# Chunked attention and a two-expert router on one core: attention and routing rewritten in a fixed engine order

## The chip, the core and the metric

One core of a Trainium2 chip runs the whole program in one launch. The metric is device time in microseconds, from the first to the last work of the core, as the median of several executions; lower is better. The core has five engines that work side by side and wait for each other by semaphores: TensorE (PE; its weight loads are PEld), VectorE (DVE), ScalarE (ACT), GpSimd (POOL) and SyncE (SP), and 16 DMA engines that all queues share. Each engine takes its instructions in order. A program on one core has no second core to wait for.

## What is computed

```python
for c in range(S // 32):                      # q, k, v: (4, 8, 768, 64), float32
    ctx = [max(0, 32*c - 16), min(S, 32*c + 32 + 8))
    k_full = concat(mem_k, k[:, :, ctx])      # 8 memory rows, up to 56 context rows
    a = softmax(q[:, :, chunk c] @ k_full.T / 8)
    out[:, :, chunk c] = a @ concat(mem_v, v[:, :, ctx])
x = out.transpose(0, 2, 1, 3).reshape(3072, 512)
nl = x @ w_gate + log1p(exp(x @ w_noise)) * noise   # (3072, 8)
for each token: its two largest nl choose two experts, with softmax weights g
y = sum over the two: g * (relu(x @ w1[e]) @ w2[e])  # w1: (8, 512, 1024), w2: (8, 1024, 512)
```

## The kernel before

Two stages follow each other, and between them tokens are sorted by the pair of experts that they chose.

**Attention.** `NPAIR` = 16 steps `n`: 4 batches by 4 pairs of heads (head `hp` on partitions 0 to 63, head `hp + 4` on 64 to 127). `load_group` (L253) brings float32 q, k and v for two pairs by POOL's queue, one group ahead of use, and broadcasts the 8 memory rows of v to all 24 chunks by SP's queue (L282). `qkT` (L333) turns q and k with 12 float32 transposes (L342), four ACT copies bring them to bf16 (L343), and POOL writes the two margins of kT (L344, L345). `scores` (L348) makes 48 small matmuls for the context (L356) and 48 for the memory (L362) into one PSUM tile per head, and for each head apart a maximum, a subtraction (DVE, L367, L369) and an exponential (ACT, L370). `probT` turns P (L377) and copies it (L379). `cast_v` (L285) makes bf16 of v, by turns on DVE and POOL (L290, L292). `mix` (L384) multiplies with v (48 matmuls, L394), divides (L398, L399) and writes bf16 rows of x.

**Routing.** After each batch `dispatch` (L126) turns x (L133, L135), makes the logits (L137), finds the top two (L139 to L157), the pair's bucket among `NB` = 28 (L163 to L170), its rank in the bucket by matmuls with triangular ones (L173 to L186), the slot (L200 to L204), and POOL scatters each tile of 128 rows of x, with gates and token number behind it, to its slots in DRAM (L227). A bucket has 128 slots; the rows beyond go to 32 spill rows. All slots were first filled with blanks by one large DMA (`fill_blank`, L87). The order within each engine comes from a scheduler that goes by priority, not from the order of the lines.

**Experts.** For each expert `e`, `load_w` (L434) casts w1 and w2 to bf16 on the way (two buffers each). `fetch` (L448) reads a bucket's 128 rows by SP, turns them (L453, one PSUM buffer `p_t`), copies them (L454) and takes gates and token numbers (POOL, L455, L456). `hidden` (L504) multiplies w1 with the 7 buckets of `e` (groups of 4 and 3, with the spill rows) and applies relu on ACT (L516) and DVE (L518). Then per bucket 8 matmuls with w2 (L547); the first expert of a pair scales into `acc` (ACT, L551), the second adds to it (DVE, L553), and POOL scatters the 128 rows to the output (L554). The spill rows follow (L560 to L565), at the end their scatter (L566), and a loop (L575) for more spill, which these inputs do not enter.

Of the kernel before, what the change touches and what calls it, by code (L numbers as in the profile page):

```python
# [17 lines left out]
Act = mybir.ActivationFunctionType  # L18


@with_exitstack
def kernel(
# [20 lines left out]

# [3 lines left out]
    assert moe_w1.shape == (E, Dm, F)  # L47
    assert moe_w2.shape == (E, F, Dm)
# [15 lines left out]
    SPILL = 32
    I32 = mybir.dt.int32
    XC = Dm // 2
    META = 8
    ROW = XC + META
    NROW = NB * CAP + N
    PAD_TOK = 4 * N  # L70
# [4 lines left out]

    xd = nc.dram_tensor("x_by_pair", [NROW, ROW], I32, kind="Internal").ap()
    xd_tile = dram_disjoint_views(xd, NP)
    out_tile = dram_disjoint_views(out, NB + 1)

    rcon = ctx.enter_context(tc.tile_pool(name="rcon", bufs=1))  # L80
    rpool = ctx.enter_context(tc.tile_pool(name="rpool", bufs=2))

    def fill_blank():
        blank = rcon.tile([128, ROW], I32, name="blank")
        nc.vector.memset(blank, 0)
        nc.vector.memset(blank[:, XC:XC + 1].bitcast(F32), float(PAD_TOK))
        nc.sync.dma_start(  # L87
            out=xd[:NB * CAP, :].rearrange("(p g) r -> p g r", p=128),
            in_=blank.rearrange("p (o r) -> p o r", o=1).to_broadcast([128, NB, ROW]),
        )  # L90
        nc.sync.dma_start(out=xd[NB * CAP:NB * CAP + SPILL, :], in_=blank[:SPILL, :])

    upper = rcon.tile([128, 128], BF16, name="upper")
    nc.gpsimd.memset(upper, 1.0)
    nc.gpsimd.affine_select(out=upper, in_=upper, compare_op=Alu.is_gt, fill=0.0, base=0, pattern=[[1, 128]], channel_multiplier=-1)
    ones = rcon.tile([128, 128], BF16, name="ones")
    nc.gpsimd.memset(ones, 1.0)

    ramp_i = rcon.tile([128, NB], I32, name="ramp_i")
    nc.gpsimd.iota(ramp_i, pattern=[[1, NB]], base=0, channel_multiplier=0)  # L100
    ramp = rcon.tile([128, NB], F32, name="ramp")
    nc.vector.tensor_copy(ramp, ramp_i)
    code = rcon.tile([128, E], F32, name="code")
    nc.vector.tensor_scalar(out=code, in0=ramp[:, :E], scalar1=-1.0, scalar2=float(E), op0=Alu.mult, op1=Alu.add)
    tok_i = rcon.tile([128, NP], I32, name="tok_i")
    nc.gpsimd.iota(tok_i, pattern=[[128, NP]], base=0, channel_multiplier=1)

    wgn_f = rcon.tile([128, KP, 2, E], F32, name="wgn_f")
    nc.sync.dma_start(out=wgn_f[:, :, 0, :], in_=moe_w_gate.rearrange("(kp p) e -> p kp e", p=128))
    nc.sync.dma_start(out=wgn_f[:, :, 1, :], in_=moe_w_noise.rearrange("(kp p) e -> p kp e", p=128))  # L110
    wgn = rcon.tile([128, KP, 2 * E], BF16, name="wgn")
    nc.vector.tensor_copy(wgn, wgn_f.rearrange("p k t e -> p k (t e)"))
    nz_all = rcon.tile([128, NP, E], F32, name="nz_all")
    nc.sync.dma_start(out=nz_all, in_=moe_noise.rearrange("(t p) e -> p t e", p=128))

    seen = rcon.tile([128, NB], BF16, name="seen")
    nc.gpsimd.memset(seen, 0.0)
    seen_ov = rcon.tile([128, 1], BF16, name="seen_ov")
    nc.gpsimd.memset(seen_ov, 0.0)
    n_spill_i = rcon.tile([128, 1], I32, name="n_spill_i")  # L120
    n_spill = rcon.tile([128, 1], F32, name="n_spill")

    def bc(ap, n):
        return ap.rearrange("p (t o) -> p t o", o=1).to_broadcast([128, BT, n])

    def dispatch(b, xrow):  # L126
        T = lambda name, shape, dt=F32: rpool.tile(shape, dt, name=name)
        t0 = b * BT
        ps_l = psR.tile([128, BT, 2 * E], F32, name="ps_l", tag="rt")
        for t in range(BT):  # L130
            p_x = psT.tile([128, KP, 128], BF16, name="p_x", tag="tr")
            for kp in range(KP):
                nc.tensor.transpose(out=p_x[:, kp, :], in_=xrow[:, t, kp * 64:(kp + 1) * 64].bitcast(BF16), identity=identb)  # L133
            xt = rpool.tile([128, KP, 128], BF16, name="xt")
            nc.scalar.copy(xt, p_x)  # L135
            for kp in range(KP):
                nc.tensor.matmul(out=ps_l[:, t, :], lhsT=xt[:, kp, :], rhs=wgn[:, kp, :], start=(kp == 0), stop=(kp == KP - 1))  # L137
        ns = T("ns", [128, BT, E])
        nc.scalar.activation(out=ns, in_=ps_l[:, :, E:], func=Act.Exp)  # L139
        nc.scalar.activation(out=ns, in_=ns, func=Act.Ln, bias=1.0)  # L140
        nl = T("nl", [128, BT, E])
        nc.vector.tensor_mul(nl, ns, nz_all[:, t0:t0 + BT, :])
        nc.vector.tensor_tensor(out=nl, in0=nl, in1=ps_l[:, :, :E], op=Alu.add)

        codeb = code.rearrange("p (o e) -> p o e", o=1).to_broadcast([128, BT, E])
        c = [T("c1", [128, BT]), T("c2", [128, BT])]
        m = [T("m1", [128, BT]), T("m2", [128, BT])]
        eq = T("eq", [128, BT, E])
        nl2 = T("nl2", [128, BT, E])
        for i, src in enumerate((nl, nl2)):  # L150
            nc.vector.tensor_reduce(out=m[i], in_=src, axis=AX, op=Alu.max)
            nc.vector.tensor_tensor(out=eq, in0=src, in1=bc(m[i], E), op=Alu.is_equal)
            nc.vector.tensor_mul(eq, eq, codeb)
            nc.vector.tensor_reduce(out=c[i], in_=eq, axis=AX, op=Alu.max)
            if i == 0:
                nc.vector.tensor_tensor(out=eq, in0=codeb, in1=bc(c[0], E), op=Alu.is_equal)
                nc.vector.scalar_tensor_tensor(out=nl2, in0=eq, scalar=-1e30, in1=nl, op0=Alu.mult, op1=Alu.add)  # L157

# [485 lines left out]
```

## Time and profile before

| what | us |
|---|---|
| median of 3 runs (482.41, 482.56, 488.23) | 482.56 |
| span of the profiled execution, first to last instruction | 478.0 |
| median less that span (start and end around it) | 4.56 |

The page shows one profiled execution, in microseconds from the start of its span. Its own time outside the profiler is not listed apart; its span and the 4.56 us around it are taken for it, so that sums made on its durations are compared with 482.56 us.

### The profile page before, as it was taken

Reading aid. Unit: us, or ns where it says so; the run is one execution under the profiler, and the core shown is the slowest. Engines: PE = TensorE matmul, PEld = TensorE weight load, DVE = VectorE, ACT = ScalarE, POOL = GpSimd, SP = SyncE. Lnnn points to the kernel's source line nnn. Section 1 sums busy time; section 2 is a strip of 40 time slices with the busy share of each in tenths; the row PEclk is TensorE's granted clock in tenths of the full one; section 3 lists DMA queues with packets and bytes.
Section 4 is the critical chain, followed back from the end, with each engine's and each line's share of the span. In section 5 each row is a group of like instructions: output and inputs, shape, how many; then the busy total and the mean of one; then the engine's idle time right before and its main releaser. Section 6 shows DMA issues by size and latency. Waiting matters only on the chain. (4 is left out here: it accounts for less than half of the span.)

```text
span 478.0 us, 10565 instructions
## 1 busy us (share of the span) xinstructions
PE 322.1 (67%) x4481; PEld 199.1 (42%) x4497; DVE 171.6 (36%) x493; ACT 127.4 (27%) x233; POOL 165.2 (35%) x267
## 2 busy tenths in 40 slices
PE   2225555454555484510399599599899999999992
PEld 2114444344444363400254265264455545454541
DVE  1014437565346468440230231231324323333341
ACT  2212232623352244500033123132231223131200
POOL 9756562179317810651100100200303140313133
PEclk9999985965556566555599789899999999999998
DMA  7999998139922800299315615715835665761112
GB/s 136 261 294 282 293 224 178 48 99 209 237 55 86 203 6 3 71 191 226 86 33 90 121 36 88 137 30 88 172 61 123 100 148 87 161 110 73 40 57 86
DMA packets 41842, 60.06 MB, mean 126 GB/s; under 512 B 14170, under 2 KB 29623, under 8 KB 41792
## 3 DMA queue, kind: packets, MB, share of 16 engines
q0 software_dynamic: 23008, 49.93, 47.0%
q1 hardware_dynamic: 18464, 9.35, 8.9%
q8 instruction: 37, 0.61, 0.6%
q14 instruction: 13, 0.11, 0.1%
q10 hardware_dynamic: 320, 0.07, 0.1%
HBM read 62.73 MB, written 14.47 MB: 162 GB/s over the span
## 5 line engine op out<-in xcount | busy, mean ns | idle before, releaser
L512 PE MATMUL ps_h<-xTb,w1t 128*128 128x384 bf16 (+4 forms) x832 | 112.8, 292 | 1.0 <-DVE xTb L454 1.0
L547 PE MATMUL ps_y<-w2t,ht 128*128 128x512 bf16 x432 | 97.1, 379 | 0.9
L512 PEld LDWEIGHTS <-w1t 128*128 128x128 bf16 x832 | 62.0, 99 | 44.3 <-issue 3.7
L516 ACT ACTIVATE ht<-ps_h 128x512 bf16<-128x512 f32 x64 | 38.2, 597 | 133.6 <-PE ps_h L512 133.6
L547 PEld LDWEIGHTS <-ht 128*128 128x128 bf16 x448 | 43.2, 98 | 51.5
L518 DVE TENSOR_SCALAR ht<-ps_h 128x416 bf16<-128x416 f32 x64 | 37.9, 592 | 65.2 <-PE ps_h L512 65.2
L554 POOL DMA_INDIRECT out_dram<-acc,tid x28 | 28.1, 1003 | 78.4 <-DVE acc L553 41.0
L553 DVE SCALAR_TENSOR_TENSOR acc<-ps_y,meta,acc 128x512 f32<-128x512 f32 x28 | 21.0, 751 | 54.5 <-PE ps_y L547 54.5
L227 POOL DMA_INDIRECT x_by_pair<-xrow,slot_i x24 | 24.5, 1023 | 37.3 <-DVE vwin L292 15.1
L551 ACT ACTIVATE acc<-ps_y,meta 128x512 f32<-128x512 f32 x28 | 19.2, 687 | 61.3 <-PE ps_y L547 61.3
L342 PE MATMUL p_t<-ident,qn 128*128 128x128 f32 x96 | 22.5, 393 | 13.8 <-DMA qn<-in_q_dram 11.8
L370 ACT ACTIVATE P<-sd 128x384 bf16<-128x384 f32 x32 | 15.7, 522 | 54.4 <-DVE sd L369 54.4
L343 ACT CAST qT<-p_t 128x384 bf16<-128x384 f32 x32 | 15.1, 479 | 42.8 <-PE p_t L342 42.4
L356 PE MATMUL ps_s<-kT,qT 64*32 64x56 bf16 x768 | 13.9, 219 | 16.7 <-POOL kT L344 5.7
L437 POOL DMA_DIRECT2D w1t<-in_moe_w_dram x8 | 6.4, 801 | 54.1 <-PE ps_h L512 54.1
L280 POOL DMA_DIRECT2D vf<-in_v_dram x16 | 22.8, 1426 | 6.2 <-issue 5.6
L342 PE MATMUL p_t<-ident,kn 128*128 128x128 f32 x96 | 21.0, 380 | 5.6 <-DMA kn<-in_k_dram 5.6
L455 POOL COPY meta<-xl 128x8 f32<-128x8 f32 x28 | 5.3, 190 | 55.7 <-DMA xl<-x_by_pair 55.6
L367 DVE TENSOR_REDUCE mx<-ps_s 128x6 f32<-128x384 f32 x32 | 16.4, 550 | 21.6 <-PE ps_s L362 18.8
L453 PE MATMUL p_t<-identb,xl 128*128 128x128 bf16 x112 | 13.0, 250 | 15.3 <-DMA xl<-x_by_pair 10.5
L342 PEld LDWEIGHTS p_t<-ident,qn 128*128 128x128 f32 x96 | 16.3, 203 | 15.3 <-issue 12.5
L362 PE MATMUL ps_s<-mkT,qT 64*32 64x8 bf16 x768 | 10.4, 176 | 16.8 <-issue 16.8
(139 smaller groups left out, 379.3 us busy)
## 6 DMA issues: line engine op xcount, KB each, us to landing
vf<-in_v_dram POOLq DMA_DIRECT2D x14, 672.0 KB, 14.4
w1t<-in_moe_w_dram POOLq DMA_DIRECT2D x8, 1024.0 KB, 8.4
w2t<-in_moe_w_dram POOLq DMA_DIRECT2D x8, 1024.0 KB, 11.1
qn<-in_q_dram POOLq DMA_DIRECT2D x14, 384.0 KB, 11.8
kn<-in_k_dram POOLq DMA_DIRECT2D x14, 384.0 KB, 11.8
x_by_pair<-blank SPq DMA_DIRECT2D x1, 3696.0 KB
xl<-x_by_pair SPq DMA_DIRECT2D x28, 132.0 KB
vf<-in_mem_v_dram SPq DMA_DIRECT2D x32, 48.0 KB
```

The costliest lines, as they stand in the source:

```text
L227: nc.gpsimd.indirect_dma_start(out=xd_tile[t0 + t], out_offset=bass.IndirectOffsetOnAxis(ap=slot_i[:, t:t + 1], axis=0), in_=xrow[:, t, :] ...
L280: nc.gpsimd.dma_start(out=dst[:, lo:hi, :], in_=src(lo, hi - lo))
L342: nc.tensor.transpose(out=p_t[:, t * 128:(t + 1) * 128], in_=src[:, hp % HV, g * HT + t, :, :], identity=ident)
L367: nc.vector.tensor_reduce(out=mx, in_=ps[hh], axis=AX, op=Alu.max)
L370: nc.scalar.activation(out=P[:, :, hh, :], in_=sd, func=Act.Exp, scale=scale)
L512: nc.tensor.matmul(out=ps_h[:, off:off + n], lhsT=w1t[:, kp, f * 128:(f + 1) * 128], rhs=rhs(kp), start=(kp == 0 and i == 0), stop=(kp == ...
L516: nc.scalar.activation(out=ht[:, f, lo:hi], in_=ps_h[:, :hi - lo], func=Act.Relu)
L518: nc.vector.tensor_scalar(out=ht[:, f, lo:hi], in0=ps_h[:, :hi - lo], scalar1=0.0, scalar2=None, op0=Alu.max)
L547: nc.tensor.matmul(out=ps_y, lhsT=ht[:, f, j * CAP:(j + 1) * CAP], rhs=w2t[:, f, :], start=(f == 0), stop=(f == FB - 1))
L551: nc.scalar.activation(out=acc[p], in_=ps_y, func=Act.Copy, scale=gate)
L553: nc.vector.scalar_tensor_tensor(out=acc[p], in0=ps_y, scalar=gate, in1=acc[p], op0=Alu.mult, op1=Alu.add)
L554: nc.gpsimd.indirect_dma_start(out=out_tile[p], out_offset=bass.IndirectOffsetOnAxis(ap=tid[p][:, 0:1], axis=0), in_=acc[p], in_offset=Non ...
```

## The change

All of the function is rewritten and emitted as written, engine by engine in the order of the lines (`manual_schedule`); nothing reorders it. What changes:

- **Loads.** POOL's DMAs cast q, k and v to bf16 on the way. q and k come as six rows of a head per piece (partition `p` holds tokens `6p` to `6p+5`, 1,536 source bytes), v as before in rows of 64 elements (256 source bytes, now 128 bytes written). `cast_v`, the margins of kT, the broadcast of the memory rows and the blank fill are gone; v's memory rows are one small load (`memv`). Each group is loaded two groups ahead (three buffers).
- **Heads.** A pair is two neighbouring heads. q and k are turned by 24 bf16 matmuls with the identity, and the copy puts tokens back in order; the memory part of scores and of P·V takes 12 matmuls over 128 queries each instead of 48 over 32. Maximum, subtraction, exponential, reciprocal and product each take both heads in one operation. Missing context is set to -1e30 by small matmuls.
- **Loop.** One iteration `i` holds: turn P of pair `i-1`, turn q and k of pair `i+2`, P·V of `i-1`, scores of `i+1`, turn x and logits of `i-2`; routing steps are put behind it, at most three per iteration (a fourth where a batch ends).
- **Routing.** Rows of x go to DRAM in token order, by SP. The table of tokens per bucket and rank is made by one-hot products on PE (`Rn`, `oht`, `ohp`, `ps_t`), summed over batches. One ACT table is loaded ahead for all functions.
- **Experts.** POOL gathers the rows of a bucket by that table (`gather`) for the next expert; they are turned between the matmuls with w2 of the present one (`turn`). Weights have three buffers, relu takes ACT and DVE by turns with four PSUM buffers, and the spill rows come after the second bucket.

```diff
+            qg = ap_.tile([128, 2 * GP, SJ * D], BF16, name="qg", bufs=3)
+            kg = ap_.tile([128, 2 * GP, SJ * D], BF16, name="kg", bufs=3)
+            vg = ap_.tile([128, GP, ncnk, D], BF16, name="vg", bufs=3)
...
+            for dst, src in ((qg, q), (kg, k)):
+                nc.gpsimd.dma_start(out=dst[:, hs, :], in_=src[b, h0:h0 + 2 * GP][hs].rearrange("h (p j) d -> p h (j d)", p=128))
...
+                        nc.gpsimd.dma_start(
+                            out=vg[p0 + j:p0 + j + nj, x, c:c + n, :],
+                            in_=bass.AP(v.tensor, v.offset + (hd * S + c * chunk + j - left_ctx) * D, [[D, nj], [chunk * D, n], [1, D]]))
...
+        new_group(0)
+        load_qk(0, 0)
+        identb = const.tile([128, 128], BF16, name="identb")
+        make_identity(nc, identb)
+        load_v(0, 0)
...
+        def qkT_pe(n):
+            g, i = divmod(n, GP)
+            qg, kg, _ = groups[g]
+            SH = SJ // 2
+            for nm, src in (("qT", qg), ("kT", kg)):
+                dst = ap_.tile([128, 128, SJ], BF16, name=nm, bufs=3)
+                for x in range(2):
+                    p_t = psT.tile([128, SH, 128], F32, name="p_t", tag="tr")
+                    for j in range(SH):
+                        for hh in range(2):
+                            nc.tensor.matmul(out=p_t[64 * hh:64 * hh + 64, j, :], lhsT=src[:, 2 * i + hh, (SH * x + j) * D:(SH * x + j + 1) * D],
+                                             rhs=identb, start=True, stop=True)
+                    nc.scalar.copy(dst[:, :, SH * x:SH * (x + 1)], p_t.rearrange("d j p -> d p j"))
...
+        def scores_pe(n):
+            b, hp = divmod(n, HP)
+            qT, kT = st[n]["qT"], st[n]["kT"]
+            ps = psS.tile([128, 2, 512], F32, name="ps_s")
+            for u in range(BT):
+                for hh in range(2):
+                    hs = slice(64 * hh, 64 * hh + 64)
+                    nc.tensor.matmul(out=ps[:, hh, u * CTX + WIN:(u + 1) * CTX], lhsT=qT[hs, 128 * u:128 * (u + 1)],
+                                     rhs=mkT[hs, hp, b * n_mem:(b + 1) * n_mem], start=True, stop=True)
...
+            mx = ap_.tile([128, 2, BT], F32, name="mx")
+            nc.vector.tensor_reduce(out=mx, in_=st[n]["ps"], axis=AX, op=Alu.max)
...
+            po = psO.tile([128, 2, 512], F32, name="ps_o")
+            OW = D + 2
+            for u in range(BT):
+                for hh in range(2):
+                    hs = slice(64 * hh, 64 * hh + 64)
+                    nc.tensor.matmul(out=po[:, hh, u * OW:u * OW + D + 1], lhsT=PT[hs, u, :], rhs=memv[hs, n, :D + 1],
+                                     start=(u == 0), stop=False, skip_group_check=True)
...
+        def xT_pe(n):
+            b, hp = divmod(n, HP)
+            p_x = psT.tile([128, BT, 128], BF16, name="p_x", tag="tr")
+            for t in range(BT):
+                nc.tensor.transpose(out=p_x[:, t, :], in_=xrows[b][:, t, hp * 64:(hp + 1) * 64].bitcast(BF16), identity=identb)
+            xt = ap_.tile([128, BT, 128], BF16, name="xt")
+            nc.scalar.copy(xt, p_x)
+            st[n]["xt"] = xt
+        def logits_pe(n):
+            b, hp = divmod(n, HP)
+            if hp == 0:
+                logits[b] = psL.tile([128, BT, 2 * E], F32, name="ps_l")
+            for t in range(BT):
+                nc.tensor.matmul(out=logits[b][:, t, :], lhsT=st[n]["xt"][:, t, :], rhs=wgn[:, hp, :],
...
+                nc.sync.dma_start(out=rows(lo, ROW, xd_part[b]), in_=xrows[b][:, :, lo:ROW])
...
+                for t in range(BT):
+                    nc.vector.tensor_scalar(out=Rn[:, t, :], in0=ramp, scalar1=rank_all[:, t0 + t:t0 + t + 1], scalar2=None, op0=Alu.is_equal)
...
+            def s6():
+                ps_t = psT.tile([128, NB], F32, name="ps_t", tag="tr")
+                for t in range(BT):
+                    for j, o in enumerate(R["ohs"]):
+                        nc.tensor.matmul(out=ps_t, lhsT=R["Rn"][:, t, :], rhs=o[:, t, :], start=(t == 0 and j == 0),
...
+        for i in range(NPAIR + 2):
+            if 0 <= i - 1 < NPAIR:
+                PT_pe(i - 1)
+            if i < NPAIR:
+                max_dve(i)
+            if i + 2 < NPAIR:
+                qkT_pe(i + 2)
+            if 0 <= i - 1 < NPAIR:
+                PT_dve(i - 1)
+            if i < NPAIR:
+                sub_dve(i)
+            if 0 <= i - 1 < NPAIR:
+                PV_pe(i - 1)
+            if i + 1 < NPAIR:
+                scores_pe(i + 1)
+            if 0 <= i - 1 < NPAIR:
+                mult_dve(i - 1)
+                if i - 1 == NPAIR - 2:
+                    nc.sync.dma_start(
+                        out=xd_part[B][(B - 1) * S:, :XC - 64].rearrange("(t p) r -> p t r", p=128),
+                        in_=xrows[B - 1][:, :, :XC - 64])
+            if 0 <= i - 2 < NPAIR:
+                xT_pe(i - 2)
+                logits_pe(i - 2)
+                if (i - 2) % HP == HP - 1:
+                    pending.extend(route((i - 2) // HP))
+                    steps(1)
+            if i % GP == 0 and i // GP >= 1 and i // GP + 2 < NG:
+                g = i // GP + 2
+                new_group(g)
+                if g == NG - 1:
+                    for x in range(GP):
+                        load_qk(g, x)
+                        load_v(g, x)
+                else:
+                    load_qk(g)
+                    load_v(g)
+            if i == 2 * (NG - 2) - 1:
+                load_w1(0)
+                load_w2(0)
+                load_w1(1)
+            if i < NPAIR:
+                steps(3)
+        steps(len(pending))
...
+        def gather(p):
+            xl = ld.tile([128, ROW], I32, name="xl")
+            nc.gpsimd.indirect_dma_start(
+                out=xl, out_offset=None, in_=xd, in_offset=bass.IndirectOffsetOnAxis(ap=gidx[:, p:p + 1], axis=0),
+                bounds_check=N - 1, oob_is_err=True)
+            got[p] = xl
...
+        def turn(p):
+            xl = got[p]
+            p_t = psX.tile([128, KP, CAP], BF16, name="p_t")
             for kp in range(KP):
+                nc.tensor.transpose(out=p_t[:, kp, :], in_=xl[:, kp * 64:(kp + 1) * 64].bitcast(BF16), identity=identb)
+            nc.vector.tensor_copy(xTv[:, :, p, :], p_t)
...
+                parts = [big[:2], big[2:], small]
+                off = 0
+                for x, ps in enumerate(parts):
+                    for p in ps:
+                        turn(p)
+                    if x == 2:
+                        turn_spill()
+                    first(W1[e], ht, off, ps, x == 2)
+                    off += len(ps) * CAP
...
+            nxt = list(plan[e + 1]) if e + 1 < E else []
+            for p in nxt:
+                gather(p)
+            if e + 2 < E:
+                load_w1(e + 2)
+            order = big + small
+            for j, p in enumerate(order):
+                second(e, p, ht, j, W2[e])
+                for _ in range(2 if j else 0):
+                    if nxt:
+                        turn(nxt.pop(0))
+                if j == 1:
+                    second_spill(e, ht, W2[e])
...
+            while nxt:
+                turn(nxt.pop(0))
+            if e + 2 < E:
+                load_w2(e + 2)
```

`route` also has steps s1 to s5 (top two, one-hot `oh` by shifted products, rank, gates) and s7, s8 (adding the table, counting what was seen). After the loop the table becomes gather indices (`gidx`), and the spill rows get theirs by 25 and 96 small matmuls on PE, which stand ahead of the first `turn`.

## Rows read from the trace of the kernel before

**Rows 1.** The page, part 1: busy time of each engine and instructions.
```profile
span 478.0 us, 10565 instructions
PE 322.1 (67%) x4481; PEld 199.1 (42%) x4497; DVE 171.6 (36%) x493; ACT 127.4 (27%) x233; POOL 165.2 (35%) x267
```

**Rows 2.** Windows by stage: length, busy per engine, PEclk, DMA share, GB/s.
```profile
37.20:194.00 156.80, 85.42 (x2744) 70.77 (x2743) 86.59 (x291) 56.49 (x117) 73.74 (x102) 0.67 0.59 145
194.00:237.40 43.40, 8.19 (x96) 6.15 (x86) 10.44 (x58) 6.42 (x11) 17.03 (x32) 0.50 0.75 154
237.40:469.30 231.90, 218.89 (x1615) 114.70 (x1628) 70.45 (x123) 57.46 (x92) 44.96 (x85) 0.95 0.46 93
```

**Rows 3.** Timeline of PE, attention: start, duration [idle before, releaser].
```profile
37.25 0.59 PE L356 MATMUL ps_s<-kT,qT 64*32 64x56 bf16 x48 [3.94 <-POOL kT L344]
...
40.85 0.82 PE L377 MATMUL p_p<-identb,P 128*128 128x128 bf16 x6
...
179.59 0.51 PE L377 MATMUL p_p<-identb,P 128*128 128x128 bf16 x6
...
191.68 0.82 PE L377 MATMUL p_p<-identb,P 128*128 128x128 bf16 x6
```

**Rows 4.** Windows around the last two of rows 3; columns as in rows 2.
```profile
178.00:181.00 3.00, 2.29 (x53) 1.73 (x52) 0.00 (x0) 2.62 (x7) 0.00 (x0) 1.00 0.00 0
190.00:193.00 3.00, 1.38 (x15) 1.03 (x15) 2.76 (x14) 0.70 (x2) 0.00 (x0) 0.50 0.00 0
```

**Rows 5.** Waits: total us, times, longest us ("issue": nothing the profile shows).
```profile
PE ps_s L362 <- issue: 16.8, 5, 5.4
...
PE ps_o L394 <- issue: 5.9, 2, 5.2
```

**Rows 6.** Groups by line: busy us, mean ns of one, idle before.
```profile
L367 DVE TENSOR_REDUCE mx<-ps_s 128x6 f32<-128x384 f32 x32 | 16.4, 550 | 21.6 <-PE ps_s L362 18.8 <-PE ps_o L394 2.7
...
L370 ACT ACTIVATE P<-sd 128x384 bf16<-128x384 f32 x32 | 15.7, 522 | 54.4 <-DVE sd L369 54.4
L343 ACT CAST qT<-p_t 128x384 bf16<-128x384 f32 x32 | 15.1, 479 | 42.8 <-PE p_t L342 42.4
...
L379 DVE COPY PT<-p_p 128x768 bf16<-128x768 bf16 x16 | 8.9, 556 | 12.4 <-PE p_p L377 12.4
...
L186 DVE TENSOR_REDUCE rank<-rk 128x6 f32<-128x168 f32 x4 | 1.3, 326 | 0.1
```

**Rows 7.** Windows: float32 loads in attention, a casting weight load.
```profile
42.00:44.00 2.00, 0.02 (x1) 0.00 (x0) 0.27 (x1) 0.00 (x0) 2.00 (x3) 1.00 1.05 346
...
258.00:260.00 2.00, 2.00 (x11) 0.88 (x9) 0.00 (x0) 0.81 (x2) 0.00 (x0) 1.00 1.13 210
```

**Rows 8.** The page, parts 3 and 6: queue q1, scatters to landing.
```profile
q1 hardware_dynamic: 18464, 9.35, 8.9%
...
x_by_pair<-xrow,slot_i POOLq DMA_INDIRECT x24, 2.9
```

**Rows 9.** Timeline between the stages.
```profile
208.73 0.16 DVE L204 TENSOR_TENSOR slot_i<-slot,spl 128x6 int32<-128x6 f32 x1
...
228.18 0.32 SPq L487 DMA_DIRECT2D s_x<-x_by_pair  x1
...
237.46 1.48 PE L512 MATMUL ps_h<-xTb,w1t 128*128 128x512 bf16 x3
```

**Rows 10.** Timeline of PE, experts.
```profile
267.26 0.38 PE L453 MATMUL p_t<-identb,xl 128*128 128x128 bf16 x4 [0.51 <-DVE xTb L454]
...
443.57 13.07 PE L512 MATMUL ps_h<-xTb,w1t 128*128 128x512 bf16 x96
456.49 12.25 PE L547 MATMUL ps_y<-w2t,ht 128*128 128x512 bf16 x54
468.67 0.63 PE L560 MATMUL ps_s<-w2t,ht 128*32 128x128 bf16 x32
```

**Rows 11.** Timeline, the last work.
```profile
471.09 0.98 POOL L566 DMA_INDIRECT out_dram<-s_acc,s_row  x1 [0.31 <-DVEq L575]
```

More of the change, by code (lines that the diff above doesn't have):

```diff
@@ L93 @@
[L93 to L110, printed above, removed]
@@ L458, in spill_gates @@
[L458 to L470 removed]
+    xd = nc.dram_tensor("x_rows", [N, ROW], I32, kind="Internal").ap()
@@ L509, in hidden, with first @@
+        def first(w1t, ht, off, ps, spill):
+            cols = [(lambda kp, z=z: xTv[:, kp, z[0]:z[-1] + 1:(z[1] - z[0] if len(z) > 1 else 1), :], len(z) * CAP) for z in runs(ps)] if ps else []
+            if spill:
+                cols.append((lambda kp: xTs[:, kp, :], SPILL))
+            n = sum(w for _, w in cols)
+            for f in range(FB):
+                ps_h = psH.tile([128, 512], F32, name="ps_h")
                 for kp in range(KP):
-                    off = 0
-                    for i, (rhs, n) in enumerate(pieces):
-                        nc.tensor.matmul(out=ps_h[:, off:off + n], lhsT=w1t[:, kp, f * 128:(f + 1) * 128], rhs=rhs(kp),
+                    o = 0
+                    for i, (rhs, w) in enumerate(cols):
+                        nc.tensor.matmul(out=ps_h[:, o:o + w], lhsT=w1t[:, kp, f * 128:(f + 1) * 128], rhs=rhs(kp),
@@ L545, with second @@
+                        o += w
+                relu(ht[:, f, off:off + n], ps_h[:, :n])
+        def second(e, p, ht, j, w2t):
             ps_y = psY.tile([128, Dm], F32, name="ps_y")
@@ L557 @@
-        ps_s = psX.tile([128, CAP], F32, name="ps_s2")
-        for f in range(FB):
-            for j in range(4):
-                nc.tensor.matmul(out=ps_s[32 * j:32 * j + 32, :], lhsT=ht[:, f, SP0:], rhs=w2t[:, f, j * 128:(j + 1) * 128],
-                                 start=(f == 0), stop=(f == FB - 1))
-        if e == 0:
-            nc.vector.tensor_scalar(out=s_acc, in0=ps_s, scalar1=gs[:, e:e + 1], scalar2=None, op0=Alu.mult)
-        else:
-            nc.vector.scalar_tensor_tensor(out=s_acc, in0=ps_s, scalar=gs[:, e:e + 1], in1=s_acc, op0=Alu.mult, op1=Alu.add)
@@ new lines, in second, with second_spill @@
+                    in_=a, in_offset=None, bounds_check=N - 1, oob_is_err=False)
+                free.append(acc[p])
+        SP0 = (E - 1) * CAP
+        def second_spill(e, ht, w2t):
+            ps_s = psX.tile([128, CAP], F32, name="ps_s2")
+            for f in range(FB):
+                for j in range(4):
+                    nc.tensor.matmul(out=ps_s[32 * j:32 * j + 32, :], lhsT=ht[:, f, SP0:], rhs=w2t[:, f, j * 128:(j + 1) * 128],
+                                     start=(f == 0), stop=(f == FB - 1))
+            if e == 0:
+                nc.vector.tensor_scalar(out=s_acc, in0=ps_s, scalar1=s_meta[:, e:e + 1], scalar2=None, op0=Alu.mult)
+            else:
+                nc.vector.scalar_tensor_tensor(out=s_acc, in0=ps_s, scalar=s_meta[:, e:e + 1], in1=s_acc, op0=Alu.mult, op1=Alu.add)
```

884 lines of the change are left out of this document (435 added, 449 removed).

## The prediction

> **What bounds the kernel now.** First the page's busy times [rows 1]: no engine is busy for more than 67% of the span, so the limits must be looked for stage by stage. The windows by stage [rows 2] show three regimes. In the experts (237.4 to 469.3) PE is busy for 218.9 of 231.9 us: PE is the bound. In the loop of attention (37.2 to 194.0) PE is busy for 85.4 and DVE for 86.6 of 156.8 us: nobody is the bound, and the time goes into waits between engines. Between the stages (194.0 to 237.4) PE works 8.2 of 43.4 us, in which the last batch is routed, scattered and read back.
>
> The timeline of attention [rows 3] shows the first scores at 37.25, held by POOL's copy of kT's margin, which stood behind POOL's DMA issues and casts. From the first P turned (40.85) to the last (191.68) 15 pairs pass at 10.06 us each; the last two took 12.09 together, 6.05 each. So one pair can go by in some 6 us; the other 4 are waits. Some of them have no cause in the profile ("issue"): two lines alone have 22.7 us in 7 halts, 3.2 us each [rows 5].
>
> The profiled execution is taken as its span, 478.0 us, and 4.6 us around it; that equals the median 482.6. Sums below are in the span.
>
> **The change, part by part.**
>
> *To the first scores.* q and k of pair 0 are POOL's first work, the cast, the margins and the blanks are gone. But PE is in order: `qkT_pe(1)` stands ahead of `scores_pe(0)`, and the second half group is issued behind four DMAs and the identity. At some 1 us an issue [rows 11] and 3 us to landing [rows 8] I place q and k of pair 1 at 13 and scores of pair 0 at 15.5 (37.8 before). Iterations 0 and 1 still wait for group 1 and fill the pipeline: 26 us to iteration 2.
>
> *One iteration.* DVE merged: an operation on 384 columns takes 0.550 and one on 168 takes 0.326 [rows 6], 1.04 ns a column; one on 768 lies between 0.55 and 1.10, and 384 more columns at 1.04 ns give 0.95, which I take. DVE: maximum 0.95, copy of PT 0.56 as now, subtraction 0.95, product 0.95, reciprocal 0.2: 3.6 us. ACT: four copies of 0.48, exponential 0.84 (bounds 0.52 and 1.04), copy of x 0.84: 3.6 us. Neither bounds a 6 us iteration. PE in its order: turn x 0.51 to 0.82 [rows 3]; a wait of 1.1 for ACT's copy of x, because the logits stand right behind; logits 0.4; turn P 0.35 to 0.65; 24 matmuls of q and k; P·V; scores. Six turns of 128 columns in 0.51 or 0.82 are at most 0.14 each, so the 24 cost 3.3 one behind the other and 1.2 where the two heads run beside each other; I take 1.5 to 2.1. P·V and scores are 48 small matmuls of 0.6 each [rows 3] and 12 wide ones of about 0.5: 1.0 each. Sum: 0.5+1.1+0.4+0.35+1.5+0.9+1.0 = 5.75 at the upper speed, 0.8+1.1+0.5+0.65+2.1+1.1+1.2 = 7.45 at the lower. I take 6.3, near the 6.05 that the old loop reached unhindered: 13 iterations (2 to 14) 82 us. What hides DVE's 3.6 is PE's chain: the next scores need the subtraction, done some 4 us into it, and reach it at 4.6.
>
> *Which speed.* Six turns took 0.51 where the granted clock was 1.00 (2.4 GHz), and 0.82 where it was 0.50 (1.2 GHz) [rows 3, 4]; PE had been busy 2.29 of 3 us around the one, 1.38 around the other. In the loop the granted clock averaged 0.67 [rows 2] with PE busy 54%. The new chain leaves PE idle for about 1.1 of 6.3 us, so I count on the upper level for most of it, not for all.
>
> *Routing inside the loop, batches 0 to 2.* s1 to s4 are put behind one iteration. PE reaches the ranks' matmuls and must wait until DVE has done s1 to s3: about 18 operations between 0.16 [rows 9] and 0.33 [rows 6], near 0.2 each, 3.6 us, and on ACT three small ones and their handovers, 0.9. About 4.5 us per batch are not covered, since P of the next pair stands behind on PE: 13.5 us (3 each would be 9; with the table's 12 matmuls and their one-hots uncovered too, 20). Next to the 42 or so small operations per batch that `dispatch` issues and POOL's six scatters (6 us of issue, nothing waited for them but the last) this is no gain in work; the gain is that POOL no longer blocks.
>
> *Halts in issue.* As many small matmuls are issued as before (about 2,800 against 2,744 in the old loop [rows 2]). Halts fell where the DMA engines were full. The blanks and float32 writes are gone, weights come in at the end. I take, against those 7, 4 halts of 3.1: 12 us (bounds: none; ten, 31).
>
> *Loads.* q and k are 12.6 MB of source in 1.5 KB pieces, v 11 MB in 43,008 pieces of 256 bytes. Before, such pieces came at 346 GB/s at a share of 1.05 [rows 7]: 16 x 1.05 x 256 / 346 = 12.4 ns per piece and engine. A casting weight load moved 210 GB/s written, so 420 read, at a share of 1.13: 372 at 1. So q and k cost about 34 us, and v 33 at 12.4 ns. Above, q1's packets, many of them 256 bytes long, held their engines for 8.9% of 478 x 16 / 18,464 = 36.9 ns [rows 8]: v 99. I take 18 ns, nearer the first row, which is v's own kind: 48, in all 82 us under 115 us of loop. Hidden, two groups ahead; at 36.9 ns the loads, 133 us from 5 on, would end some 23 us late.
>
> The Trainium skill (DMA: Bandwidth & Descriptors, Specifications) says that a transfer needs at least 512 bytes for full rate and that a smaller write is a read and a write, which speaks against v's 128 bytes. The trace does not bear it out at 256 bytes (346 GB/s); no row shows 128. If it doubled v's 48 us, loads would end at 135 and the sum be some 20 us longer.
>
> *End of attention.* Last iterations without q, k and scores: 9 us to the last logits. Sum so far: 26 + 82 + 13.5 + 12 + 9 = 142.5.
>
> *Between the stages.* Last routing, s1 to s7 in a row: about 0.9 ACT, 24 DVE operations (5.5), ranks 0.9, table 1.2, handovers: 9 us (dispatch took from 194 to 208.9). Then the gather, about 1 us of issue each [rows 11] and 2.9 to land; but 121 small matmuls for the spill stand ahead of the first turn on PE, with DVE steps between: 7 us, then two turns 2: 9 us. What goes: the scatter and the wait for it beside four weight loads (208.9 to 228.2), and the reads and first turns (228.2 to 237.5) [rows 9]. First expert matmul at 160.5, not 237.5: 77 us gained.
>
> *Experts.* One expert that waits for nothing takes 443.57 to 456.49 to 468.67 and 0.6: 25.66 us [rows 10]; eight 205.3. Before 231.9, so 26.6 went to bucket reads, turns and the start [rows 2]. After: 21 turns between matmuls, 0.24 each, 5.0; of two in a row the second waits for the copy out of the one `p_t`: 0.51 [rows 10] at least, 1.2 behind an addition on DVE: 9 times 0.82, 7.4. Expert 0 works in three parts and waits for turns: 7.8. Sum 225.5, a gain of 6.4. Weights, three buffers, are hidden by a whole expert. POOL's gathers (1.3 each) stand ahead of the next weight load, which has 25 us.
>
> *Tail.* The spill's scatter [rows 11] is no longer last: 8.0 instead of 8.7.
>
> Total: 142.5 + 9 + 9 + 225.5 + 8.0 = 394 us of span, 398.6 with the 4.6 around it: **399 us**, faster by 84.
>
> **Rivals.**
>
> 1. *PE stays at 2.4 GHz and halts vanish.* Iterations of 5.75 (-7), no halts (-12), routing 3 per batch (-4.5): 375 us. For: emptier DMA queues, POOL free. Against: every batch stops PE for some microseconds.
> 2. *The loop keeps its old pace.* If in-order waits put 10.06 us [rows 3] on each of 13 iterations, routing and halts included (forecast: (82+13.5+12)/13 = 8.3): +23, 422 us. For: nothing in the loop had a busy bound, and a hand-made order has stops of its own. Against: the 6.05 of the last pairs.
> 3. *Expert stage does not gain.* If gathers or double turns cost as much as the old reads, and POOL's longer list delays weights: 232 + 5 instead of 225.5: 410 us. Against: gathers are issued a whole expert ahead.
> 4. *Slower: v's 128-byte pieces bound.* One mechanism: a fixed price per piece of a casting load. Loads end at 5 + 34 + 43,008 p / 16, and attention needs them by 115 in the forecast. To lose the 84 gained and 2% more it takes 93 us late, p = 63 ns; at 100 ns the sum is 592 us. For: no row shows 128-byte writes. Against: q1's mean of 36.9 and v's own 12.4 ns. The skill's rule above points this way, but its doubling gives 36 ns, not 63.
> 5. *The fixed order does not take effect where it matters*, an instruction still waits for the old engine: as 2, or about 440 with POOL's queue late.
>
> **How the numbers follow.** Forecast (386 to 408) 0.45; rival 1 0.2; rival 2 0.17; rival 3 0.1; rival 5 0.04; rival 4 0.04. Rival 1 with 3 us off the experts gives 372; iterations at 7.45 (+15) and ten halts (+19) give 433. The range is **372 to 434**; it leaves out rival 4 and the ends. Two per cent, about what a measurement of this kernel can tell from no change, is 472.9 to 492.2: faster 0.93, same 0.03, slower 0.04.
>
> **What would show it.** Right: first maximum near 15 us; pairs 6 to 7 us apart with a stop of 4 to 5 us per batch before the ranks' matmuls; no DMA wait of PE after iteration 2; first w1 matmul near 160; experts 1 to 6 within 2 to 4 us of 25.7. Wrong: halts "issue" above 20 us; pairs 8 us apart without routing; PE waiting for v or k; a DMA share near 1 all through attention; turns waiting for gathers.

## The result, and the profile after

The changed kernel took 414.06 us (median of 4 runs, 412.89 to 414.79) against 484.18 for the kernel before beside it: ratio 0.8528, 95% interval 0.8478 to 0.8578. The forecast of 399 (372 to 434) named the right side, and its range holds the measured time, but it lay 15 us low. The profiled execution took 414.79 us, its span 413.1.

First the windows of the changed kernel by stage (columns as in [rows 2]), then PE's turns of P, which answer to [rows 3]:

```profile
34.40:158.00 123.60, 78.69 (x2512) 61.88 (x2512) 74.08 (x178) 52.32 (x93) 30.27 (x34) 0.58 0.89 111
158.00:175.40 17.40, 4.78 (x149) 3.76 (x149) 10.32 (x54) 1.09 (x5) 4.24 (x4) 0.50 0.15 37
175.40:402.80 227.40, 217.34 (x1658) 118.41 (x1675) 75.62 (x132) 58.06 (x123) 65.36 (x66) 0.98 0.49 102
```
```profile
34.46 0.51 PE L259 MATMUL p_p<-identb,P 128*128 128x128 bf16 x6
...
41.07 0.82 PE L259 MATMUL p_p<-identb,P 128*128 128x128 bf16 x6
...
151.56 0.80 PE L259 MATMUL p_p<-identb,P 128*128 128x128 bf16 x6
```

Set beside [rows 2, 3, 9 and 11], the 64.9 us of span come from four places: the first P is turned 6.4 us earlier, the 15 pairs after it take 117.1 instead of 150.8 (-33.7), from the last P to the first matmul with w1 it is 23.9 instead of 45.8 (-21.9), the experts take 4.5 less, and the tail 1.6 more. The two stages that got much shorter are those in which [rows 2] showed no busy engine. PE's work hardly shrank (page, part 1, against [rows 1]), and VectorE issues a quarter fewer instructions:

```profile
span 413.1 us, 10205 instructions
...
PE 307.4 (74%) x4522; PEld 189.5 (46%) x4540; DVE 164.1 (40%) x377; ACT 119.4 (29%) x235; POOL 124.2 (30%) x141
```

The timeline of the start shows where the forecast missed. POOL works in order and makes the constants behind all loads of three groups; DVE's cast of `ramp` waits for them, DVE's copy of `ident` stands behind that cast, and PE's first instruction behind the copy. q and k of pair 0 had been issued at 1.35 and 2.25.

```profile
25.61 0.23 POOL L170 IOTA ramp_i<- 128x128 int32 x1
...
25.87 0.24 DVE L172 CAST ramp<-ramp_i 128x128 bf16<-128x128 int32 x1 [24.01 <-POOL ramp_i L170]
...
26.33 0.16 DVE L186 CAST ident<-identb 32x32 f32<-32x32 bf16 x1
...
26.55 0.63 PE L195 MATMUL p_m<-ident,mk_nat 32*128 32x32 f32 x4 [26.55 <-DVE ident L186]
...
31.52 0.96 DVE L245 TENSOR_REDUCE mx<-ps_s 128x12 f32<-128x768 f32 x1 [5.02 <-PE ps_s L237]
```

The waits between 30 and 160 us (total, times, longest) hold the loop's stops: x's copy in every iteration, the ranks in three batches, and 6 halts ("issue": PE stands, and the profile shows nothing that it waits for) of 8.4 us in all. The loop before had 10 of 31.3 us, 7 of them in the two lines of [rows 5]. The groups answer to [rows 6]:

```profile
PE ps_l L311 <- ACT xt L303: 14.7, 16, 0.9
...
PE ps_r L366 <- DVE oh L361: 8.7, 2, 4.4
...
PE ps_r L366 <- DVE ge L377: 4.5, 1, 4.5
...
PE ps_s L234 <- issue: 3.6, 2, 2.1
...
PE ps_o L281 <- issue: 2.8, 3, 1.6
...
PE p_p L259 <- issue: 2.0, 1, 2.0
```
```profile
L214 ACT CAST qT<-p_t 128x384 bf16<-128x384 f32 x32 | 17.2, 593 | 30.7 <-PE p_t L212 30.7
...
L303 ACT COPY xt<-p_x 128x768 bf16<-128x768 bf16 x16 | 12.8, 799 | 23.4 <-PE p_x L301 23.4
...
L245 DVE TENSOR_REDUCE mx<-ps_s 128x12 f32<-128x768 f32 x16 | 15.2, 951 | 7.2 <-PE ps_s L237 7.2
```

Between the stages (timeline, as [rows 9]) the second gather stands 3.4 us on POOL, by my reading because its buffer lies in memory that `sone` used (with `sone` elsewhere, in the run together, it waits 0.30, but so it does with v uncast, where `sone` was not moved); in the experts the second of two turns waits as in [rows 10]; the last scatter [rows 11] now leaves 9.3 us to the end instead of 6.9:

```profile
165.84 0.18 DVE L504 TENSOR_SCALAR gidx<-tab 128x28 int32<-128x28 f32 x1
...
171.44 1.04 POOL L572 DMA_INDIRECT xl<-x_rows,gidx  x1 [3.40 <-PE p_t L581]
...
175.43 1.86 PE L636 MATMUL ps_h<-xTb,w1t 128*128 128x256 bf16 x8 [0.52 <-DVE xTb L582]
...
206.69 0.38 PE L581 MATMUL p_t<-identb,xl 128*128 128x128 bf16 x4 [1.11 <-DVE xTb L582]
...
403.80 0.98 POOL L652 DMA_INDIRECT out_dram<-acc,sidx  x1 [0.74 <-DVEq L730]
```

### The profile page after: what moved, and what is told of

Same layout as the page of the kernel before. It is cut to its first block, busy times and chain, and to the rows that moved or that the text cites. A ratio compares the mean times of both kernels' runs of the same rounds, so it can differ in the third digit from the quotient of the medians.

```text
span 413.1 us, 10205 instructions
## 1 busy us (share of the span) xinstructions
PE 307.4 (74%) x4522; PEld 189.5 (46%) x4540; DVE 164.1 (40%) x377; ACT 119.4 (29%) x235; POOL 124.2 (30%) x141
## 4 chain that ended last, share of the span: by engine, by line
PE 65%; DVE 10%; issue 10%; ACT 5%; DMA 5%; POOL 3%; POOLq 0%; DVEq 0%; ACTq 0%
PE ps_h L636 23%; PE ps_y L644 20%; PE p_t L212 5%; DMA vg<-in_v_dram 4%; ACT xt L303 3%; PE p_x L301 2%; PE ps_o L281 2%; PE p_t L581 2%; PE p_p L259 2%; PE ps_o L275 2%; PE ps_s L234 2%; ACT qT L214 2%; POOL out_dram L652 2%; DVE xTb L582 1%; PE ps_l L311 1%
## 5 line engine op out<-in xcount | busy, mean ns | idle before, releaser
L636 PE MATMUL ps_h<-xTb,w1t 128*128 128x512 bf16 (+3 forms) x608 | 109.4, 330 | 1.1 <-DVE xTb L582 1.0
L624 DVE TENSOR_SCALAR ht<-ps_h 128x416 bf16<-128x416 f32 (+2 forms) x68 | 41.7, 613 | 82.9 <-PE ps_h L636 80.9
L652 POOL DMA_INDIRECT out_dram<-acc,sidx x28 | 28.0, 999 | 144.9 <-DVE acc L651 142.4
L622 ACT ACTIVATE ht<-ps_h 128x416 bf16<-128x416 f32 (+2 forms) x68 | 36.4, 535 | 80.8 <-PE ps_h L636 75.6
L117 POOL DMA_DIRECT2D vg<-in_v_dram x34 | 33.0, 975 | 61.0 <-PE ps_o L281 58.3
L572 POOL DMA_INDIRECT xl<-x_rows,gidx x28 | 29.2, 1041 | 68.2 <-DVE ov1b L515 46.6
L636 PE MATMUL ps_h<-xTs,w1t 128*128 128x32 bf16 x256 | 45.9, 179 | 0.2 <-issue 0.2
L303 ACT COPY xt<-p_x 128x768 bf16<-128x768 bf16 x16 | 12.8, 799 | 23.4 <-PE p_x L301 23.4
L212 PE MATMUL p_t<-identb,kg 128*64 128x128 bf16 x192 | 15.1, 285 | 4.2 <-ACT qT L214 3.7
L214 ACT CAST kT<-p_t 128x384 bf16<-128x384 f32 x32 | 17.5, 610 | 2.1 <-PE p_t L212 2.1
L245 DVE TENSOR_REDUCE mx<-ps_s 128x12 f32<-128x768 f32 x16 | 15.2, 951 | 7.2 <-PE ps_s L237 7.2
L311 PE MATMUL ps_l<-wgn,xt 128*128 128x16 bf16 x96 | 5.2, 176 | 14.7 <-ACT xt L303 14.7
```

What stands on the lines that cost most here:

```text
L117: nc.gpsimd.dma_start(out=vg[p0 + j:p0 + j + nj, x, c:c + n, :], in_=bass.AP(v.tensor, v.offset + (hd * S + c * chunk + j - left_ctx) * D, ...
L212: nc.tensor.matmul(out=p_t[64 * hh:64 * hh + 64, j, :], lhsT=src[:, 2 * i + hh, (SH * x + j) * D:(SH * x + j + 1) * D], rhs=identb, start= ...
L214: nc.scalar.copy(dst[:, :, SH * x:SH * (x + 1)], p_t.rearrange("d j p -> d p j"))
L572: nc.gpsimd.indirect_dma_start(out=xl, out_offset=None, in_=xd, in_offset=bass.IndirectOffsetOnAxis(ap=gidx[:, p:p + 1], axis=0), bounds_c ...
L622: nc.scalar.activation(out=dst, in_=src, func=Act.Relu)
L624: nc.vector.tensor_scalar(out=dst, in0=src, scalar1=0.0, scalar2=None, op0=Alu.max)
```

## The experiments

All runs, by four points of each trace (us): P of pairs 0 and 1 turned, `gidx` made, first matmul with w1; then the median, and the ratio to the kernel before of the same chip. That kernel took 480 us beside the first four, 485 beside the next four, 481 to 483 beside the rest, so small differences are read inside a group or from the traces.

| Run | P 0 | P 1 | gidx | w1 | us | ratio [95%] |
|---|---|---|---|---|---|---|
| changed kernel, first | 34.5 | 41.1 | 165.8 | 175.4 | 414.1 | 0.853 [0.848, 0.858] |
| constants first | 23.4 | 29.8 | 156.8 | 165.5 | 402.1 | 0.840 [0.834, 0.845] |
| ident first | 28.4 | 34.8 | 157.9 | 166.6 | 406.4 | 0.848 [0.843, 0.853] |
| half v | 29.6 | 35.1 | 159.0 | 167.6 | 400.9 | 0.835 [0.829, 0.840] |
| own order | 21.2 | 27.9 | 159.4 | 167.1 | 405.4 | 0.846 [0.841, 0.852] |
| changed kernel, again | 34.0 | 40.6 | 165.2 | 174.9 | 413.2 | 0.850 [0.843, 0.858] |
| x early | 33.5 | 40.3 | 160.6 | 170.3 | 409.6 | 0.843 [0.836, 0.850] |
| ranks later | 33.5 | 40.4 | 158.7 | 168.3 | 408.2 | 0.840 [0.833, 0.847] |
| single turns | 33.8 | 40.1 | 166.1 | 175.8 | 406.6 | 0.836 [0.830, 0.843] |
| v uncast | 42.4 | 53.0 | 190.7 | 198.4 | 434.7 | 0.900 [0.891, 0.908] |
| per head | 33.4 | 40.2 | 165.9 | 175.7 | 412.6 | 0.855 [0.849, 0.861] |
| together | 23.1 | 29.4 | 145.7 | 153.0 | 382.1 | 0.793 [0.788, 0.799] |
| together, half v | 20.4 | 26.7 | 137.7 | 145.0 | 375.9 | 0.782 [0.779, 0.785] |

**The start.** POOL's constants, with DVE's casts of them and `ident`, move ahead of the loads of v of pair 1 and of all later ones.

```diff
         load_qk(0, 1)
+        upper = const.tile([128, 128], BF16, name="upper")
...
+        nc.vector.tensor_copy(ident, identb[:32, :32])
         load_v(0, 1)
```


> The routing constants of POOL and DVE and the copy of ident move ahead of v of pair 1 and of groups 1 and 2. Theory (the start's order alone made the 15 us that the forecast missed): ident's copy at about 9 instead of 26.3 us, first turn on PE at 9 to 11, scores of pair 0 ended at 15 to 17, those of pair 2 at 26; the kernel at 399 to 403 us, and all later steps of the same length. Rival (the start is bound by loading, 1.62 of the DMA engines being busy up to 26.5 us): scores of pair 0 come early, but PE then waits for q, k or v of groups 0 and 1 and pair 2 is reached at 35 or later: 408 to 414 us.

The first maximum comes at 14.23, near the 15 of the forecast. But P of pair 0 is turned at 23.37 and pair 1's at 29.77, 11.3 earlier than in the changed kernel, where the forecast missed 15. The timeline shows the rival's wait in the place of the one removed:

```profile
14.23 0.96 DVE L245 TENSOR_REDUCE mx<-ps_s 128x12 f32<-128x768 f32 x1 [4.23 <-PE ps_s L237]
...
17.42 0.85 PE L212 MATMUL p_t<-identb,qg 128*64 128x128 bf16 x12 [3.25 <-DMA qg<-in_q_dram]
...
21.00 0.85 PE L212 MATMUL p_t<-identb,kg 128*64 128x128 bf16 x12 [2.73 <-DMA kg<-in_k_dram]
```

So both hold in part: the order costs 11 us, and behind it q and k of pair 2, which stand behind v in POOL's queue, make PE wait 3.25 and 2.73 us. At `gidx` 9 of the 11 are left.

```diff
         make_identity(nc, identb)
+        ident = ap_.tile([32, 32], F32, name="ident", bufs=1)
+        nc.vector.tensor_copy(ident, identb[:32, :32])
```


> Only DVE's copy of ident moves, to right behind the identity; the constants stay behind the loads. Theory (POOL's order holds DVE too): PE turns pairs 0 and 1 and scores pair 0 by 15 to 17 us, but DVE's first maximum stands behind the cast of ramp, at 26 instead of 31.4: 5 us gained, 408 to 410 us. Rival (only the order on DVE ahead of PE matters): as much as with the constants moved, 399 to 403 us.

The first P comes 6 us earlier, near the 5 of the theory, since the first maximum stands behind the late constants (25.47); at `gidx` it is 7.9. In ratio alone this run does not part from the changed kernel; its trace does. Beside it, constants first turns P of pair 1 5.0 us earlier but makes `gidx` only 1.1 earlier (it has halts of 9.6 us, this run 6.1). So by the traces the copy of `ident` alone carries most of what is left at `gidx`; the medians lie 4.3 us apart.

**v's pieces.** Half of v's chunks are not loaded.

```diff
-                    piece(int(first), ncnk - first - last)
+                    piece(int(first), ncnk // 2 - first)
...
-                                     rhs=vg[hs, i, c, :], start=False, stop=True, skip_group_check=True)
+                                     rhs=vg[hs, i, c % (ncnk // 2), :], start=False, stop=True, skip_group_check=True)
```


> Half of v's chunks are not loaded (the others are used twice), so half of the 43,008 pieces go. Theory (v's pieces hide behind the loop; of the start they hold POOL's constants by the waits in its queue, 3.1 us and shorter issues): 409 to 412 us, the loop from the scores of pair 2 to those of pair 15 stays at 103 us (101 to 104). Rival (v's pieces bound the loop, the DMA engines' share being 1.05 there): the loop falls to 90 to 95 us, 395 to 402 in all. The share of the queue of casting loads falls by the price of a piece: at 18 ns by 21,500 x 18 / (16 x 410 us) = 6 points, at 57 ns by 19.

Part 3 of its page:

```profile
q0 software_dynamic: 50416, 36.09, 55.8%
```

Against 67.1% of 401.9 us in the run with ident first: 16 x (0.671 x 401.9 - 0.558 x 400.8) = 737 us of engine time for 21,504 pieces, 34 ns each. This is an estimate: the last two runs give 38 by the same sum, and among runs with all loads share times span goes from 267.7 to 279.4 us. The time, 400.9, lies in the rival's range, but not by the rival's cause: from P 1 to `gidx` it takes 123.9 us against 124.8, so v's pieces do not bound the loop here. They do set the start (P 0 4.9 earlier), and the halts of the three lines above fall from 8.4 to 3.7 us. Why the loop did not get shorter by as much is not shown; one difference is TensorE's granted clock, 0.50 on average from 34.4 to 158 against 0.58 in the changed kernel.

**The order.** The same operations, left to the scheduler of the language.

```diff
-    with tc.manual_schedule():
-        kept = body()
+    kept = body()
```


> The same operations, without the fixed order: the scheduler of the language orders them, as in the kernel before. Theory (part of the gain is the order): the loop comes back towards the old pace of 10 us a pair, and work for later stands ahead of work that is due: 425 to 445 us. Rival (the operations carry the gain alone): 410 to 418 us.

The theory fell: 405.4 us, ratio 0.846, no slower than the fixed order. It starts 13 us earlier: neither `ident`'s copy nor the first maximum stands behind the constants (10.0 instead of 31.5). From the first P to the first matmul with w1 it then takes 145.9 us, 4.9 more than the fixed order's 141.0. One long stop there is 9.8 us, where DVE's product waits for the DMA of rows out of `xrow`:

```profile
DVE xrow L293 <- DMA x_rows<-xrow: 9.8, 1, 9.8
```

So the operations carry the gain without the fixed order. What the order earns behind the start, some 5 us by these two traces, its own late start loses again.

**The changed kernel again,** beside the next three.

> The changed kernel itself, beside the others. On the chip of the first four runs the kernel before took 480 us against 484 on the first chip, so 409 to 414 us here; its span split as in the first profile: first work of PE at 26.5, gidx at 164 to 166, first w1 matmul at 173 to 176 us. If the fixed order is worth what the run in the language's own order (405 us, ratio 0.846) says, this comes out no faster than that: ratio 0.846 to 0.856.

All as expected: 413.2 us, ratio 0.850, and the same four points within 0.6 us.

**PE's wait for x.**

```diff
+            if 0 <= i - 2 < NPAIR:
+                xT_pe(i - 2)
             if i + 1 < NPAIR:
                 scores_pe(i + 1)
...
-                xT_pe(i - 2)
                 logits_pe(i - 2)
```


> The turns of x stand one block earlier on PE, ahead of the scores, and the logits stay behind the scores, so that ACT's copy of x (0.80 us) lies beside the scores. Theory (PE's chain in its order is the bound of an iteration): the wait of 0.89 us goes in each of 14 iterations, 10 to 12 us less than the changed kernel. Rival (an iteration is bound by the chain maximum, subtraction, exponential, turn through three engines): PE then waits elsewhere, 0 to 4 us less.

The wait goes from 14.7 us in 16 times to 2.8 in 3, but the kernel is only 3.7 us shorter:

```profile
PE ps_l L311 <- ACT xt L303: 2.8, 3, 0.9
```

The rival's time holds (0 to 4 us less): most of PE's wait covered another wait. Which one is not shown iteration by iteration.

**The stops ahead of the ranks.**

```diff
+            def s3b():
                 ohb = R["oh"][:, :, :NB]
                 ps_r = psT.tile([128, BT, NB], F32, name="ps_r", tag="tr")
...
-                steps(3)
+                steps((1, 2, 3, 3)[(i + 3) % HP])
```


> The routing's steps are spread: s1 and s2 behind the batch's last logits, s3 (DVE part) and s4 one iteration later, the ranks' matmuls two, the table three. Theory (the stop of 4.4 us on PE ahead of the ranks is a wait for DVE in a fixed order and can be covered): the three stops inside the loop fall below 0.5 us, 9 to 12 us less than the changed kernel. Rival (DVE's small operations delay the next maximum by as much wherever they stand): 0 to 4 us less, with PE waiting for PT or P instead.

The three stops inside the loop go (the one left is the last batch's), and 5.0 us are won, between the two theories. The waits of this kernel show what took the place: 7.5 us for PT, which stands on DVE behind the routing (2.0 before), and 8.9 for ACT's copies of qT (4.5 in the changed kernel beside it).

```profile
PE ps_o L275 <- DVE PT L264: 7.5, 5, 3.4
...
PE ps_r L368 <- DVE oh L361: 4.4, 1, 4.4
```

**Two turns in a row.**

```diff
-                for _ in range(2 if j else 0):
+                for _ in range(1 if j else 0):
```


> One turn of a gathered bucket behind each second product, never two in a row. Theory (the second of two turns waits 0.5 to 1.1 us for the copy out of the one p_t): 9 such waits go, 5 to 8 us less than the changed kernel, experts 0 to 4 alone shorter. Rival (PE's granted clock pays the pauses back, or the last turn's copy now stops the next expert's first product): 0 to 2 us.

6.6 us less in the median. In the traces the experts take 220.1 instead of 225.7 in the changed kernel beside it (227.4 in its first trace), and the waits for the copy fall from 8.7 us to 1.7 (6.6 in the first trace):

```profile
PE p_t L581 <- DVE xTb L582: 1.7, 2, 1.1
```

The theory holds.

**The casting load undone for v.**

```diff
+                    nc.gpsimd.tensor_copy(vb[p0:p0 + WIN, x], groups[g][2][p0:p0 + WIN, x])
...
+            if i % GP == 0 and i < NPAIR:
+                cast_v(i // GP)
```


> v is loaded as float32 (256 bytes written per piece, as in the kernel before) and POOL casts each group one iteration before its use; all else as in the changed kernel. Theory (a piece of 128 bytes written costs some 34 ns by the run with half of v, one of 256 uncast 12.4): the share of the queue falls by about 43,008 x 21.6 ns / (16 x 410 us) = 14 points, POOL's constants come 3 to 5 us earlier, halts in issue get fewer: 4 to 8 us less than the changed kernel's 413 on a like chip (ratio 0.834 to 0.842). Rival (a piece has its price whatever it writes): the share stays within 3 points, time within 2 us or longer by POOL's casts.

Neither held whole: the share fell by 10 points, and the kernel is 21 us longer than the changed kernel. POOL's constants came later (30.2, not 25.1), with longer waits in its queue, and the casts stand in POOL's order ahead of the next loads:

```profile
31.09 12.20 POOL L136 CAST vb<-vg 56x1536 bf16<-56x1536 f32 x8
43.24 0.81 POOL L108 DMA_DIRECT2D qg<-in_q_dram  x1
```

The queue's time fell by 429 us (56.2% of 434.6 against 65.9% of 411.3 beside it), 10 ns per piece: about 24 uncast, 34 cast, by estimate. From P 0 to `gidx` it takes 148.3 us, 17 more than in the changed kernel, half of the 34 that the loop gained. PE waits there for no load and no cast of v; its halts are 21.5 us, against 8.7 in the run per head beside it:

```profile
PE ps_s L243 <- issue: 8.8, 4, 4.5
...
PE p_t L221 <- issue: 5.5, 2, 2.8
```

So most of the 17 us are halts. Why casts on POOL should bring them is not shown.

**The merge of two heads undone** in DVE's three large operations.

```diff
-            nc.vector.tensor_reduce(out=mx, in_=st[n]["ps"], axis=AX, op=Alu.max)
+            for hh in range(2):
+                nc.vector.tensor_reduce(out=mx[:, hh, :], in_=st[n]["ps"][:, hh], axis=AX, op=Alu.max)
```


> Maximum, subtraction and product are made per head again (two operations on 384 columns for each one on 768); nothing else changes. Theory (the merge saves only a fixed 0.15 us an operation, 2 x 0.55 against 0.95; maximum and subtraction lie on the chain to P, but DVE is busy for half of an iteration): 1 to 5 us more than the changed kernel. Rival (the merge carries a good part of the 34 us that the loop gained): 10 us more or above.

412.6 us, ratio 0.855: no difference from the changed kernel that can be measured. The merge of these three operations carries nothing that shows. So of the 34 us that the loop gained, half goes with the casting load, and none with the merge or, by the run in the language's own order, with the order alone; which of the other changes carry the rest was not tried.

**Together,** with `sone` in memory of its own.

```diff
-        sone = ap_.tile([128, NP, SPILL], BF16, name="sone", bufs=1)
+        sone = rp.tile([128, NP, SPILL], BF16, name="sone")
```


> Constants first, turns of x early, ranks later, single turns, and the one-hots of the spill in memory of their own (so that the second gather need not wait for them). Theory (the gains lie in different places and add up: 9 at the start, 4, 5, 6.5, 2 to 3): 384 to 390 us, ratio 0.79 to 0.80. Rival (an earlier start and a faster loop run into the loads): 392 to 398, with PE waiting for q, k or v and longer halts in issue.

382.1 us, 30 less than the run per head beside it: the gains add up, and this is the best of all runs that do the whole work. From `gidx` to w1 it takes 7.3 instead of 9.6; no run has the memory of `sone` changed alone, and this stretch takes 7.7 to 9.8 in runs that share it.

> The five edits together, and half of v's chunks not loaded (the others are used twice). Theory (with the start and the loop shortened, loading is the next bound of the first part: in the kernel with the five edits PE waits 6.0 us for q and k and 13 us in halts called issue up to the routing of the last batch): those waits for q and k go, halts fall to about half, 6 to 12 us less than 382 (ratio 0.768 to 0.781). Rival (the chain of engines in an iteration is the bound, and waits for loads are only displaced): 379 to 383 us, ratio 0.786 to 0.796.

Half of v's chunks are not loaded here either. 6.2 us less, at the edge of the theory: PE's waits for q and k fall from 6.0 to 3.6 us, its halts from 13.3 to 6.2. So with the five edits loading still costs the first part some 6 us.

## Why the prediction was right, and 15 us low

By its own steps, forecast against the first trace of the changed kernel:

| Step | forecast | trace |
|---|---|---|
| to iteration 2 (P 1) | 26 | 41.1 |
| from there to `gidx`: loop, routing, halts, last chain | 125.5 | 124.8 |
| index, gather, two turns | 9 | 9.6 |
| experts | 225.5 | 227.4 |
| tail | 8 | 10.3 |
| around the span | 4.6 | 1.7 |

The step that failed is "To the first scores": 15.5 for the first scores, where the maximum came at 31.5. I looked for what POOL issues ahead of q and k of pair 1, and did not follow POOL's constants through DVE to the copy that PE's first instruction needs. That is 11 of the 15 us (constants first). The other 4 are put down to the wait for pair 2's q and k that shows once the first is gone; with half of v besides, in the last run, P of pair 1 comes at 26.7, near the forecast's 26.

- *One iteration, 6.3.* Ahead of the first routing, P turns lie 5.7 to 7.0 us apart (34.5, 41.1, 47.7, 53.4, 60.4). The 13 iterations from P of pair 1 to P of pair 14 take 106.2 us; without the three stops for the ranks and the halts in them (13.2 and 6.9) that is 6.6 each. But PE's chain is not alone the bound: 12 us of its waits taken away gave 3.7.
- *Which speed.* Here the sum was lucky. I counted on the upper level for most of the loop; the granted clock averaged 0.58, and only 4 of the 16 turns of P show a length of 0.49 to 0.51. At the lower level my own sum was 7.45, but a pair there took 6.1 to 6.6, and 4.8 to 4.9 at the upper, where I had 5.75. Both sums were about a microsecond too high, the level was lower than I counted on, and the two errors cancelled.
- *Routing, 4.5 per batch.* Three stops of 4.4; as priced. *Halts,* 12: 8.4. I had read that halts fall where the DMA engines are full; of the ten before, seven did (share 1.01 to 1.27), but one fell at 0.00.
- *Loads, hidden.* Right for the loop, with too low a price: about 34 ns per piece of v, not 18, 91 us instead of 48. Of the signs of being wrong one came, a DMA share near 1 (0.89 in the loop), and did not mean that loads bound it. The price per packet of [rows 8] was no price per piece: without the cast, the queue has 28,912 packets for all loads, though v alone has 43,008 pieces, and with it 74,928. The 12.4 ns of [rows 7] came from one window of 2 us; over a whole run uncast pieces cost about 24.
- The Trainium skill (DMA: Bandwidth & Descriptors, Specifications) says that a transfer under 512 bytes is a read and a write. No run here tests that: cast pieces (128 bytes written) and uncast ones (256) both lie under 512, at about 34 and 24 ns. Twice the 18 ns that I took is 36, close to the 34, but the 20 us that I had put on it did not come.
- *Rivals.* 1 (375) and 2 (422) fell with the loop at its forecast pace; 3 fell, the experts gained 4.5; 4 fell by 34 ns against its 63; 5 came in another sense: the order earned some 5 us behind the start and lost 13 at it.

## What to carry to other kernels

Where an order is written by hand, follow the first instruction of the bounding engine back through every engine's queue, constants too: a copy that nobody prices stood here behind 25 us of DMA issues. A wait on the fullest engine is worth what the next wait leaves of it, 3.7 of 12 us here, while a wait in a stage that one engine fills came back for the most part (5.6 of 7.0 us in the experts). The cast in the load cost some 10 ns a piece, and was still 21 us cheaper than the cast on POOL. A step whose length comes out right can rest on two errors: look at its terms, not at the sum alone.

## What the runs showed of the hardware

TensorE's clock does show in the loop's pace. In the run per head, six turns of P take 0.82 us at first and 0.49 to 0.50 in the next three pairs, the lengths that [rows 3, 4] have at 0.50 (1.2 GHz) and 1.00 (2.4 GHz). From the slow turns to the next ones it took 6.60 us, and then 4.83 and 4.87, all without a halt:

```profile
40.23 0.82 PE L262 MATMUL p_p<-identb,P 128*128 128x128 bf16 x6
...
46.83 0.49 PE L262 MATMUL p_p<-identb,P 128*128 128x128 bf16 x6
...
51.66 0.49 PE L262 MATMUL p_p<-identb,P 128*128 128x128 bf16 x6
...
56.53 0.50 PE L262 MATMUL p_p<-identb,P 128*128 128x128 bf16 x6
```

Early in a trace the column PEclk does not tell this. In the run per head it reads 1.00 for the slow pair as for the two fast ones. With constants first it reads 1.00 up to 92 us, as in this window, while turns of P take 0.80 to 0.82 up to 73:

```profile
40.00:60.00 20.00, 15.16 (x492) 11.99 (x492) 9.56 (x14) 10.41 (x19) 5.52 (x6) 1.00 1.48 108
```
```profile
46.78 0.80 PE L259 MATMUL p_p<-identb,P 128*128 128x128 bf16 x6
...
52.92 0.80 PE L259 MATMUL p_p<-identb,P 128*128 128x128 bf16 x6
```

So the level is better read from an operation whose two lengths are known. The 0.67 of [rows 2] has the same fault: the column reads 1.00 up to 60 us there, while P's turn at 40.85 takes 0.82.

PE's halts called "issue" do not follow the loads alone: 3.7 and 6.2 us in the runs with half of v, 6.1 to 13.3 with all of v cast in the fixed order, but 21.8 with the same loads in the language's own order and 21.5 with v uncast. What makes them stays open.
